# First exchange of q, k and softmax weights by ScalarE copies across partitions, and one store for a block's results

## The chip, the core and the metric

The kernel is one program on one core of a Trainium2 chip. The metric is device time in microseconds (us) of one execution, from launch to end; lower is better. Engines are named as in the profile: PE (TensorE, matmuls), PEld (its weight loads), DVE (VectorE), ACT (ScalarE), POOL (GpSimd), SP (SyncE, which here issues the DMAs).

## The reference, cut to what matters

```
scores = scale * q_c @ k_c^T          # chunks of 64 tokens; B=8, H=8, S=576, D=64
attn   = exp(scores - max) / (sum + 1e-9)
x      = (attn @ v_c)  -> (4608 tokens, 512)
h = x @ w_in;  g = h * sigmoid(1.702 h);  x = g @ w_out          # 512 -> 2048 -> 512
h = x @ w_in2; g = max(h,0) + alpha*min(h,0); out = g @ w_out2   # the same sizes
```

The weights come as 64-bit floats, which ACT and DVE turn into 32-bit ones, and every matmul operand of the feed-forward layers is split into a high and a low part by ACT, DVE and POOL; so these engines have a steady side job beside the matmuls.

## The kernel before, in words

The tokens are 36 groups of 128, nine blocks of 512. The program has two stages. In the first, up to about 525 us in the profile, the first feed-forward layer runs over the first five blocks as 80 steps n (five blocks times 16 slices of the hidden width). A step is 12 matmuls into `psH` (`emit_h`, L692, matmuls L699), the activation on ACT (L709), a rounded copy on ACT (L712), a subtraction on DVE (`gs`, L717), and two steps later 12 matmuls into `psY` (`emit_y`, L722, matmuls L729). Two `psH` buffers are in turn, so step n+2 can start only when the DVE subtraction of step n is done. Around these steps the attention of all later token groups and the preparation of the second layer's weights (lines L273 to L368) are threaded in by tables: every step has two half-slots, 2n in the middle of `emit_h` and 2n+1 after `emit_y`, and `put(half_slot, function, group)` decides what is issued there. All engines take their instructions in the order in which these functions issue them. In the second stage what remains of both layers runs as block products with seven multiplications (L699/L729 give way to L975 and L1123); it has its own tables (`GROUP_OP`, `LATE_0`, `LATE_STAGE`).

The place of the change is the attention of a token group with turn i. A group's q and k are loaded with 64 tokens of one half of the heads on 64 partitions (`load_nat`, L418); DVE transposes blocks of 32x32 (`qk_T`, L438, instructions L441) into a tile `ops` of 128 partitions x 2 halves x 768 columns (512 columns of q and k of group i, and 256 columns of the transposed softmax weights of the group two turns before, L610). Since a 32x32 transpose leaves half the data on the wrong 32 partitions, an exchange follows in three steps:

- `off_copy` (L449): ACT copies half 0 of `ops`, 128 x 768, aside into `off` (one buffer).
- `off_send` (L459): per 64 partitions, half 1 of the lower 32 partitions goes to half 0 of the upper 32. Two DMAs on SP, L463.
- `off_fetch` (L465): per 64 partitions, the upper 32 partitions of `off` go to half 1 of the lower 32. Two DMAs on SP, L469. It overwrites what `off_send` reads.

There are 30 such exchanges: 26 of 768 columns, two of 512 (turns 4 and 5) and two of 256. After it PE multiplies attention weights with v (`att_PV`, L640, 32 small matmuls into `psX`) and q with k of the next group but one (L538), both from the exchanged tile; ACT takes the product out (L654), DVE takes the maximum (L559, L561), ACT the exponential (L569, with a table load before and after, because the activation of L709 needs another table), DVE normalises (L577 to L582) and transposes (L610). In half-slots from the group's entry TAU: the maximum, exponential, normalising and transposing at 1, 1, 2, 2 (`ATT_AT`), the exchange of the tile two turns on at 3, 3, 4 (`OFF_AT`), and the product at TAU of the turn two later, mostly 8.

SP is one queue: it issues all DMAs in program order and stops at each that has to wait. At the end of a block `emit_y` takes four `psY` banks out (ACT L744, DVE L742, 128x512 each) into one tile `ysb` that is also the home of the next x, and stores each quarter by a DMA of its own into `x2d`, two at this half-slot and two at the next (`send_later`, issued at L295).

```
for fn, at in zip((off_copy, off_send, off_fetch), OFF_AT):
    put(t + at, fn, i + LAG)
put(pv, att_PV, g)
```

Of the kernel before, what the change touches and what calls it, by code (L numbers as in the profile page):

```python
# [17 lines left out]
SQ = 32  # L18
# [15 lines left out]

LAG = 2
LEAD = 3
TAU = (4, 10, 16, 22, 28, 32, 36, 40, 44, 48, 52, 56, 60, 64, 68, 72, 76, 80, 84, 88, 92, 96, 100, 104, 108, 112, 116, 120, 124, 128, 132, 136)
QK_T_AT = (18, 23)
OFF_FIRST = (1, 2, 4)
QK_4 = (4, 9)  # L40
ATT_FIRST = (-3, 1, 2, 5, 6, 7)
LO_POOL_O = (0, 0, 0, 1, 0, 0, 1, 0, 1, 1, 1, 1, 1, 0, 0, 1)
LO_POOL_I = (0, 0, 0, 1, 0, 1, 0, 0, 0, 0, 1, 0, 1, 1, 0, 0)
WI_DVE = (1, 0, 1, 0)
# [2 lines left out]
KEEP_WO = 0  # L47
KEEP_FROM = 10
KEEP_AT = 3
LATE_SEND = (1, 1)  # L50
SPLIT_AT = 3
XS_POOL = (0, 1, 1, 1)

END = (6, 9)
PREP_AT = (28, 33, 38, 43, 48, 53, 58, 63, 68, 73, 78, 83, 88, 93, 98, 103, 109, 114, 119, 124, 129, 134, 139, 143, 146)
FOLD_AT = (33, 36, 40, 44, 47, 50, 54, 57, 61, 63, 69, 72, 76, 79, 82, 85, 89, 93, 96, 100, 104, 107, 110, 113, 116, 119, 123, 127, 131, 134, 138, 141)
FOLD_SEND = 1
X1_SEND = 0
YSB_SEND = 0
PREP_STAGE = (0, 3, 4, 6, 9)  # L60
LATE_STAGE = (1, 5, 5, 8, 13)
ATT_AT = (1, 1, 2, 2)
OFF_AT = (3, 3, 4)
V_AT = 0
D_AT = 1
SUMS_AT = (43, 46, 71, 74)
X_HI_AT = (3, 8, 20, 24, 33, 36, 46)
FIRST_LOAD = 29
GROUP_OP = (27, 30, 34, 36, 43, 45, 47)
GROUP_SUM = (24, 32, 29, 38)  # L70
PREP_SEND = (0, 0)
LATE_0 = (90,)
LATE_2 = (8, 20, 34)
LATE_1 = (16, 46, 74)

# [25 lines left out]
def tile_chunk_attention_two_ffn(  # L101
# [14 lines left out]
    nc = tc.nc  # L116
    B, H, S, D = q.shape
    NT, DM = out.shape
    DFF = w_in1.shape[1]
    P = 128  # L120
    CH = 64
# [38 lines left out]
    x2d = [dram.tile([P, KT, NB], F32, name=f"x2_{j}") for j in range(NBLK)]  # L160
# [128 lines left out]
    def send_later(after=1, **dma):  # L289
        waiting.append((half + after, dma))  # L290
# [140 lines left out]
    ops_t, off_t = {}, {}  # L431
# [17 lines left out]
    def off_copy(k):  # L449
        if k < GPB + LAG:  # L450
            if k == GPB:
                off_t[k + 1] = raw_p.tile([P, 2, DW], F32, tag="raw2", name="off")
            off_t[k] = off_t[GPB + 1][:, k - GPB]
        else:
            off_t[k] = off_p.tile([P, DW + PW], F32, tag="off", name="off")
        c = cols(k) if k < len(GROUP_ORDER) else slice(DW, DW + PW)
        nc.scalar.copy(off_t[k][:, c], ops_t[k][:, 0, c])

    def off_send(k):  # L459
        t = ops_t[k]  # L460
        c = cols(k) if k < len(GROUP_ORDER) else slice(DW, DW + PW)
        for r in range(0, P, CH):
            nc.sync.dma_start(out=t[r + SQ:r + CH, 0, c], in_=t[r:r + SQ, 1, c])  # L463

    def off_fetch(k):  # L465
        t, o = ops_t[k], off_t[k]
        c = cols(k) if k < len(GROUP_ORDER) else slice(DW, DW + PW)
        for r in range(0, P, CH):
            nc.sync.dma_start(out=t[r:r + SQ, 1, c], in_=o[r + SQ:r + CH, c])  # L469

    qkT = {}

# [249 lines left out]
    def emit_y(n):  # L722
        j, f = divmod(n, NF)
        if f == 0:
            y_t[j] = [ps_y.tile([P, 512], F32, tag="y", name="psY") for _ in range(4)]
        gs, w = gs_t.pop(n), wt["wo", 0, f]
        for b, a in ((0, 0),) if n in Y_WHOLE else ((0, 0), (0, 1), (1, 0)):
            for t in range(4):
                nc.tensor.matmul(  # L729
                    y_t[j][t], w[:, a, t * P:(t + 1) * P], gs[:, b],  # L730
                    start=(f == 0 and a + b == 0), stop=(f == NF - 1 and b == 1),
                )
        if f == NF - 1:
            if j < NPL - 1:
                sbs = x_p.tile([P, 4, 512], F32, tag="x", name="ysb")
            for t, ps in enumerate(y_t.pop(j)):
                if j == NPL - 1:
                    sb = wpool.tile([P, 512], F32, tag=f"wo{8 + t}", name="ysb")
                else:
                    sb = sbs[:, t]  # L740
                if t % 2:
                    nc.vector.tensor_copy(sb, ps)  # L742
                else:
                    nc.scalar.copy(sb, ps)  # L744
                if j == NPL - 1:
                    nc.sync.dma_start(out=x2d[j][:, t], in_=sb)
                else:
                    send_later(YSB_SEND + t // 2, out=x2d[j][:, t], in_=sb)

# [172 lines left out]
    def second_layer():  # L924
# [27 lines left out]
        def split_soon():  # L952
            while unsplit:
                when = clock + (4 if clock < 14 else SPLIT_AT)
                at(when, split_factor, *unsplit.pop(0))
                at(when + KEEP_AT, keep_factors)

# [294 lines left out]
    with tc.manual_schedule():  # L1252
# [72 lines left out]
        for i, g in enumerate(GROUP_ORDER):  # L1325
            t = TAU[i]
            if i < GPB:
                for fn, at in zip((att_T, att_X, att_N, att_AT, att_PV), ATT_FIRST):
                    if i > 0 or fn is not att_T:
# [3 lines left out]
                if i == 0:  # L1333
                    put(t, att_S_matmuls, g)
                put(t + ATT_FIRST[5], load_v, GROUP_ORDER[i + 1])
                continue
            pv = TAU[i + LAG] if i + LAG <= last else TAU[last] + END[i + LAG - last - 1]
            before = QK_T_AT[i - GPB] if i < GPB + LAG else TAU[i - LAG] + D_AT
            put(before - LEAD, load_nat, g)
# [135 lines left out]
```

## Time and profile before

| | |
|---|---|
| median of three runs | 1555.92 us (1552.63 to 1559.21) |
| the profiled execution: its own time | 1560.17 us |
| its span, first to last instruction | 1558.4 us |
| PE busy | 1527.9 us, 98% |
| PEld busy | 1279.3 us, 82% |
| DVE busy | 1218.7 us, 78% |
| ACT busy | 955.5 us, 61% |
| POOL busy | 568.4 us, 36% |

The profiled execution is 4.25 us above the median of the runs; 1.8 us of its time lie outside the span. "Busy" of PE is the union of modelled matmul times.

### The profile page before, as it was taken

Reading aid. Unit: us, or ns where it says so; the run is one execution under the profiler, and the core shown is the slowest. Engines: PE = TensorE matmul, PEld = TensorE weight load, DVE = VectorE, ACT = ScalarE, POOL = GpSimd, SP = SyncE. Lnnn points to the kernel's source line nnn. Section 1 sums busy time; section 2 is a strip of 40 time slices with the busy share of each in tenths; the row PEclk is TensorE's granted clock in tenths of the full one; section 3 lists DMA queues with packets and bytes.
Section 4 is the critical chain, followed back from the end, with each engine's and each line's share of the span. In section 5 each row is a group of like instructions: output and inputs, shape, how many; then the busy total and the mean of one; then the engine's idle time right before and its main releaser. Section 6 shows DMA issues by size and latency. Waiting matters only on the chain.

```text
span 1558.4 us, 25552 instructions
## 1 busy us (share of the span) xinstructions
PE 1527.9 (98%) x9169; PEld 1279.3 (82%) x9169; DVE 1218.7 (78%) x1428; ACT 955.5 (61%) x1347; POOL 568.4 (36%) x542
## 2 busy tenths in 40 slices
PE   8999999999999999999999999999999999999998
PEld 6687777787888778888888787888888888999998
DVE  6998778676774659998899778777877788778777
ACT  6777666666674566666556665565655556556653
POOL 0135655666556222221111553225222422342330
PEclk9999999999999999999999999999999999999999
DMA  9925888899888477658665985689668866997985
GB/s 258 336 56 138 237 229 249 240 252 262 234 250 244 136 215 234 199 151 284 184 183 167 304 295 178 193 201 296 190 194 210 268 189 197 258 347 239 257 270 149
DMA packets 414958, 349.59 MB, mean 224 GB/s; under 512 B 139248, under 2 KB 337520, under 8 KB 414832
## 3 DMA queue, kind: packets, MB, share of 16 engines
q1 hardware_dynamic: 414832, 347.96, 75.6%
q8 instruction: 73, 1.20, 0.3%
q14 instruction: 53, 0.43, 0.1%
HBM read 257.70 MB, written 79.17 MB: 216 GB/s over the span
## 4 chain that ended last, share of the span: by engine, by line
PE 63%; DVE 6%; DMA 3%; POOL 2%; issue 2%; ACT 1%; SPq 1%; DVEq 0%; POOLq 0%; ACTq 0%
PE psYa L1123 16%; PE psHa L975 16%; PE psYb L1123 12%; PE psHb L975 12%; PE psY L729 3%; PE psH L699 3%; DVE o L1051 1%; DVE yacc L1161 1%; DMA wo<-fold 1%; DVE g L1026 1%; DVE w L874 1%; DMA wo<-u 1%; POOL fold L333 0%; POOL fold L364 0%; DMA ops<-ops 0%
## 5 line engine op out<-in xcount | busy, mean ns | idle before, releaser
L699 PE MATMUL psH<-xs,wi 128*128 128x512 f32 x960 | 234.9, 394 | 6.0 <-DVE gs L717 4.8
L729 PE MATMUL psY<-gs,wo 128*128 128x512 f32 x912 | 224.5, 396 | 1.1 <-DVE gs L717 1.1
L1123 PE MATMUL psYa<-o,w 128*128 128x512 f32 (+1 forms) x960 | 220.0, 377 | 1.8 <-DVE o L1051 1.6
L699 PEld LDWEIGHTS psH<-xs,wi 128*128 128x128 f32 x960 | 180.0, 189 | 48.4 <-DVE gs L717 7.2
L975 PE MATMUL psHa<-xop,wi2t 128*128 128x512 f32 (+1 forms) x948 | 214.1, 374 | 1.8 <-ACT g L1014 1.8
L1123 PEld LDWEIGHTS psYa<-o,w 128*128 128x128 f32 x960 | 176.5, 188 | 32.4 <-DVE o L1051 4.1
L729 PEld LDWEIGHTS psY<-gs,wo 128*128 128x128 f32 x912 | 169.8, 189 | 38.3 <-DVE gs L717 1.5
L975 PEld LDWEIGHTS psHa<-xop,wi2t 128*128 128x128 f32 x948 | 174.5, 188 | 29.4 <-ACT g L1014 2.2
L1123 PE MATMUL psYb<-o,w 128*128 128x512 f32 (+1 forms) x744 | 168.3, 374 | 0.4 <-DVE o L1051 0.4
L975 PE MATMUL psHb<-xop,wi2t 128*128 128x512 f32 (+1 forms) x744 | 167.1, 373 | 0.0
L990 ACT ACTIVATE neg<-g 128x1024 f32<-128x1024 f32 (+1 forms) x80 | 78.1, 976 | 126.0 <-DVE g L1026 125.3
L1123 PEld LDWEIGHTS psYb<-o,w 128*128 128x128 f32 x744 | 136.9, 188 | 22.0 <-DVE o L1051 0.8
L975 PEld LDWEIGHTS psHb<-xop,wi2t 128*128 128x128 f32 x744 | 136.8, 188 | 20.7
L1056 POOL TENSOR_TENSOR tsum<-g,tsum 128x1024 f32<-128x1024 f32 (+1 forms) x38 | 98.9, 2602 | 140.3 <-DVE o L1051 104.0
L1056 POOL TENSOR_TENSOR tsum<-g,g 128x1024 f32<-128x1024 f32 (+1 forms) x19 | 42.0, 2208 | 252.5 <-DVE g L998 252.5
L1161 DVE TENSOR_TENSOR yacc<-psYb,yacc 128x1024 f32<-128x1024 f32 (+1 forms) x73 | 83.2, 1139 | 40.5 <-PE psYb L1123 40.4
L1161 DVE TENSOR_TENSOR yacc<-psYa,yacc 128x1024 f32<-128x1024 f32 (+1 forms) x86 | 97.9, 1138 | 19.3 <-PE psYa L1123 19.3
L1051 DVE TENSOR_TENSOR o<-tsum,o 128x1024 fp32r<-128x1024 f32 (+1 forms) x61 | 71.5, 1171 | 52.3 <-ACT o L1046 52.1
L998 DVE SCALAR_TENSOR_TENSOR g<-g,neg 128x1024 f32<-128x1024 f32 (+1 forms) x80 | 101.0, 1263 | 9.4 <-ACT neg L992 9.4
L992 ACT ACTIVATE neg<-neg,minus_alpha 128x512 f32<-128x512 f32 (+1 forms) x160 | 100.2, 674 | 2.6
L1023 ACT COPY g<-psHa 128x1024 f32<-128x1024 f32 (+1 forms) x56 | 53.1, 949 | 78.1 <-DVE o L1051 49.9
L717 DVE TENSOR_TENSOR gs<-psH,gs 128x512 fp32r<-128x512 f32 x76 | 51.4, 678 | 62.6 <-ACT gs L712 62.5
(180 smaller groups left out, 2854.8 us busy)
## 6 DMA issues: line engine op xcount, KB each, us to landing
w<-wo SPq DMA_DIRECT2D x140, 512.0 KB, 4.1
wi2t<-wi SPq DMA_DIRECT2D x208, 256.0 KB, 3.8
w<-wi SPq DMA_DIRECT2D x72, 256.0 KB, 3.8
w<-wo SPq DMA_DIRECT2D x56, 256.0 KB, 3.1
raw<-in_moe_w_in_dram SPq DMA_DIRECT2D x16, 512.0 KB, 6.9
raw<-in_moe_w_out_dram SPq DMA_DIRECT2D x16, 512.0 KB, 7.3
raw<-in_moe_w_in_dram SPq DMA_DIRECT2D x32, 256.0 KB, 3.8
raw<-in_moe_w_out_dram SPq DMA_DIRECT2D x32, 256.0 KB, 4.7
```

Of the source, the lines that this page charges most:

```text
L699: nc.tensor.matmul(ps, w[:, a, c], xs[:, b, c], start=(i == 0), stop=(i == 3 * KT - 1))
L717: nc.vector.tensor_tensor(out=gs[:, 1], in0=g, in1=gs[:, 0].bitcast(F32), op=ALU.subtract)
L729: nc.tensor.matmul(y_t[j][t], w[:, a, t * P:(t + 1) * P], gs[:, b], start=(f == 0 and a + b == 0), stop=(f == NF - 1 and b == 1),)
L975: nc.tensor.matmul(ps, w[:, c, a], x[b][:, c], start=(k == 0 and i in (1, 2, 5)), stop=(k == 5 and i in (2, 3, 4)), skip_group_check=True,)
L990: nc.scalar.activation(out=neg, in_=src, func=AF.Relu, scale=-1.0)
L992: nc.scalar.activation(out=neg[:, jj], in_=neg[:, jj], func=AF.Copy, scale=minus_alpha[:, f + jj:f + jj + 1])
L998: nc.vector.scalar_tensor_tensor(out=g, in0=g, scalar=0.0, in1=neg, op0=ALU.max, op1=ALU.add)
L1023: nc.scalar.copy(g({1: "11", 6: "12", 5: "22"}[i]), src)
L1051: nc.vector.tensor_tensor(out=lo, in0=wide(homes[nm], n), in1=hi.bitcast(F32), op=ALU.subtract)
L1056: eng.tensor_tensor(out=wide(homes[out], n), in0=wide(homes[x], n), in1=wide(homes[y], n), op=ALU.subtract,)
L1123: nc.tensor.matmul(ps[:, d, :n], w[:, jj, d, a], x[b][:, jj], start=(k == 0 and i in (1, 5, 2)), stop=(k == 5 and i in (3, 2, 4)), skip_gr ...
L1161: nc.vector.tensor_tensor(out=out_acc, in0=ps[:, :, :n], in1=acc, op=ALU.add)
```

## The change

Three parts. `off_send` goes through a new helper `move`, and with SEND_BY "A" its two DMAs become two ACT copies of 32 partitions each, from partitions r to r+31 to partitions r+32 to r+63; `off_fetch` stays two DMAs on SP and `off_copy` one ACT copy. The four stores of a finished block (four of the first-stage blocks, so 16 DMAs of 256 KB) become one of 1 MB each (four DMAs), issued once the fourth quarter is out. And the tables are set anew: `off_send` moves from half-slot 3 to 4 (`OFF_AT`), the entries of turns 10 to 13 in `TAU` go from even to odd half-slots (52, 56, 60, 64 to 51, 55, 59, 63), and single entries of `QK_T_AT`, `ATT_FIRST`, `END`, `FOLD_AT`, `LATE_STAGE`, `GROUP_OP` and `LATE_0` move by one or two.

```diff
--- before.py
+++ after.py
@@ -34,11 +34,11 @@
 
 LAG = 2
 LEAD = 3
-TAU = (4, 10, 16, 22, 28, 32, 36, 40, 44, 48, 52, 56, 60, 64, 68, 72, 76, 80, 84, 88, 92, 96, 100, 104, 108, 112, 116, 120, 124, 128, 132, 136)
-QK_T_AT = (18, 23)
+TAU = (4, 10, 16, 22, 28, 32, 36, 40, 44, 48, 51, 55, 59, 63, 68, 72, 76, 80, 84, 88, 92, 96, 100, 104, 108, 112, 116, 120, 124, 128, 132, 136)
+QK_T_AT = (18, 24)
 OFF_FIRST = (1, 2, 4)
 QK_4 = (4, 9)
-ATT_FIRST = (-3, 1, 2, 5, 6, 7)
+ATT_FIRST = (-3, 1, 2, 5, 6, 8)
 LO_POOL_O = (0, 0, 0, 1, 0, 0, 1, 0, 1, 1, 1, 1, 1, 0, 0, 1)
 LO_POOL_I = (0, 0, 0, 1, 0, 1, 0, 0, 0, 0, 1, 0, 1, 1, 0, 0)
 WI_DVE = (1, 0, 1, 0)
@@ -47,29 +47,33 @@
 KEEP_WO = 0
 KEEP_FROM = 10
 KEEP_AT = 3
+SEND_BY = "A"
+FETCH_BY = "S"
+OFF_BY = "A"
+YSB_ONE = 1
 LATE_SEND = (1, 1)
 SPLIT_AT = 3
 XS_POOL = (0, 1, 1, 1)
 
-END = (6, 9)
+END = (5, 9)
 PREP_AT = (28, 33, 38, 43, 48, 53, 58, 63, 68, 73, 78, 83, 88, 93, 98, 103, 109, 114, 119, 124, 129, 134, 139, 143, 146)
-FOLD_AT = (33, 36, 40, 44, 47, 50, 54, 57, 61, 63, 69, 72, 76, 79, 82, 85, 89, 93, 96, 100, 104, 107, 110, 113, 116, 119, 123, 127, 131, 134, 138, 141)
+FOLD_AT = (33, 36, 40, 44, 47, 51, 54, 57, 61, 63, 69, 72, 76, 79, 82, 85, 89, 93, 96, 100, 104, 107, 110, 113, 116, 119, 123, 127, 131, 134, 138, 141)
 FOLD_SEND = 1
 X1_SEND = 0
 YSB_SEND = 0
 PREP_STAGE = (0, 3, 4, 6, 9)
-LATE_STAGE = (1, 5, 5, 8, 13)
+LATE_STAGE = (0, 5, 5, 8, 13)
 ATT_AT = (1, 1, 2, 2)
-OFF_AT = (3, 3, 4)
+OFF_AT = (3, 4, 4)
 V_AT = 0
 D_AT = 1
 SUMS_AT = (43, 46, 71, 74)
 X_HI_AT = (3, 8, 20, 24, 33, 36, 46)
 FIRST_LOAD = 29
-GROUP_OP = (27, 30, 34, 36, 43, 45, 47)
+GROUP_OP = (28, 30, 34, 36, 43, 44, 47)
 GROUP_SUM = (24, 32, 29, 38)
 PREP_SEND = (0, 0)
-LATE_0 = (90,)
+LATE_0 = (92,)
 LATE_2 = (8, 20, 34)
 LATE_1 = (16, 46, 74)
 
@@ -454,19 +458,25 @@
         else:
             off_t[k] = off_p.tile([P, DW + PW], F32, tag="off", name="off")
         c = cols(k) if k < len(GROUP_ORDER) else slice(DW, DW + PW)
-        nc.scalar.copy(off_t[k][:, c], ops_t[k][:, 0, c])
+        move(OFF_BY, off_t[k][:, c], ops_t[k][:, 0, c])
+
+    def move(by, out, in_):
+        if by == "S":
+            nc.sync.dma_start(out=out, in_=in_)
+        else:
+            {"A": nc.scalar.copy, "D": nc.vector.tensor_copy, "P": nc.gpsimd.tensor_copy}[by](out, in_)
 
     def off_send(k):
         t = ops_t[k]
         c = cols(k) if k < len(GROUP_ORDER) else slice(DW, DW + PW)
         for r in range(0, P, CH):
-            nc.sync.dma_start(out=t[r + SQ:r + CH, 0, c], in_=t[r:r + SQ, 1, c])
+            move(SEND_BY, t[r + SQ:r + CH, 0, c], t[r:r + SQ, 1, c])
 
     def off_fetch(k):
         t, o = ops_t[k], off_t[k]
         c = cols(k) if k < len(GROUP_ORDER) else slice(DW, DW + PW)
         for r in range(0, P, CH):
-            nc.sync.dma_start(out=t[r:r + SQ, 1, c], in_=o[r + SQ:r + CH, c])
+            move(FETCH_BY, t[r:r + SQ, 1, c], o[r + SQ:r + CH, c])
 
     qkT = {}
 
@@ -744,8 +754,11 @@
                     nc.scalar.copy(sb, ps)
                 if j == NPL - 1:
                     nc.sync.dma_start(out=x2d[j][:, t], in_=sb)
-                else:
-                    send_later(YSB_SEND + t // 2, out=x2d[j][:, t], in_=sb)
+                elif YSB_ONE:
+                    if t == 3:
+                        send_later(YSB_SEND, out=x2d[j], in_=sbs)
+                elif t % 2:
+                    send_later(YSB_SEND, out=x2d[j][:, t - 1:t + 1], in_=sbs[:, t - 1:t + 1])
```

How the order of instructions changes, at three places. First ACT, at the exchange whose copy aside the trace shows at 352.98 us; before (L457 is the copy aside, L321 a rounding of a prepared weight, L709 and L712 the activation and its rounded copy, L654 the product taken out, L569 the exponential and its table, L216 the first step of a weight's preparation):

```order
L457 COPY off<-ops 128x768
L321 CAST g<-u 128x384
L709 ACTIVATE psH<-psH 128x512
L712 CAST gs<-psH 128x512
L654 COPY x<-psX 128x4x64 x2
L569 ACT_TABLE_LOAD
L569 ACTIVATE e<-e 128x512
L216 ACTIVATE u<-raw_4160 128x512
L709 ACT_TABLE_LOAD
L709 ACTIVATE psH<-psH 128x512
```

And of the change, at the same place (L467 is the line in the helper, both for the copy aside and for the send; L325, L719, L722, L664, L579 and L220 are the lines above, 4 to 10 further down):

```order
L467 COPY off<-ops 128x768
L325 CAST g<-u 128x384
L719 ACTIVATE psH<-psH 128x512
L722 CAST gs<-psH 128x512
L664 COPY x<-psX 128x4x64 x2
L467 COPY ops<-ops 32x768 x2
L579 ACT_TABLE_LOAD
L579 ACTIVATE e<-e 128x512
L220 ACTIVATE u<-raw_4151 128x512
L719 ACT_TABLE_LOAD
L719 ACTIVATE psH<-psH 128x512
```

Two copies of 32x768 stand between the product taken out and the table load of the exponential; nothing else moved on ACT here.

Then SP at the same exchange, before (L463 the send, L469 the fetch, L283 a weight's load, L295 stores, L407 the load of v):

```order
L283 DMA raw_4160<-in_moe_w_in_dram 128x2x128 x2
L463 DMA ops<-ops 32x768 x2
L295 DMA wi_6_147<-g 128x3x128
L295 DMA wi_6_147<-u 128x3x128
L407 DMA v<-in_v_dram 128x8x64
L469 DMA ops<-off 32x768 x2
L295 DMA wo_0_125<-fold 896x1x128
```

And of the change (L465 is the helper's line, here the fetch):

```order
L287 DMA raw_4151<-in_moe_w_in_dram 128x2x128 x2
L299 DMA wi_6_147<-g 128x3x128
L299 DMA wi_6_147<-u 128x3x128
L411 DMA v<-in_v_dram 128x8x64
L465 DMA ops<-off 32x768 x2
L299 DMA wo_0_125<-fold 896x1x128
```

The send's two DMAs are gone; the queue comes to the stores, v and the fetch directly from the weight's load.

Last PE, at the products of turns 9 to 11; before (L699 a step's first matmuls, L729 its second, L640 and L538 the attention):

```order
L699 MATMUL psH<-xs,wi 128x512 x12
L640 MATMUL psX<-ops,v 64x64 x16
L538 MATMUL psX<-ops 64x64 x16
L729 MATMUL psY<-gs,wo 128x512 x12
L699 MATMUL psH<-xs,wi 128x512 x12
L729 MATMUL psY<-gs,wo 128x512 x12
L699 MATMUL psH<-xs,wi 128x512 x12
L640 MATMUL psX<-ops,v 64x64 x16
L538 MATMUL psX<-ops 64x64 x16
L729 MATMUL psY<-gs,wo 128x512 x12
L699 MATMUL psH<-xs,wi 128x512 x12
```

And of the change (L709, L739, L650 and L548 in their place):

```order
L709 MATMUL psH<-xs,wi 128x512 x12
L650 MATMUL psX<-ops,v 64x64 x16
L548 MATMUL psX<-ops 64x64 x16
L739 MATMUL psY<-gs,wo 128x512 x12
L709 MATMUL psH<-xs,wi 128x512 x12
L739 MATMUL psY<-gs,wo 128x512 x12
L650 MATMUL psX<-ops,v 64x64 x16
L548 MATMUL psX<-ops 64x64 x16
L709 MATMUL psH<-xs,wi 128x512 x12
L739 MATMUL psY<-gs,wo 128x512 x12
L709 MATMUL psH<-xs,wi 128x512 x12
```

From the second product on (entry 51 in place of 52) the attention's matmuls stand ahead of the 12 matmuls of a step that they stood behind; so it is for four turns.

## Rows read from the trace of the kernel before

**Rows 1.** Who PE waited for, 160 to 364 us: total us, times, longest

```profile
PE psX L640 <- DMA ops<-off: 4.5, 6, 1.5
PE psX L640 <- DMA wi<-u: 1.1, 1, 1.1
PE psY L729 <- DVE gs L717: 1.1, 1, 1.1
PE psX L640 <- DVE d L579: 0.9, 1, 0.9
PE psH L699 <- DVE gs L717: 0.9, 2, 0.6
PE psX L640 <- DMA x<-xg: 0.6, 1, 0.6
```

**Rows 2.** PE in order of time: start, us, what, [idle before, releaser]

```profile
183.16 0.80 PE L640 MATMUL psX<-ops,v 64*64 64x64 f32 x30 [1.09 <-DMA wi<-u]
...
220.93 0.83 PE L640 MATMUL psX<-ops,v 64*64 64x64 f32 x30 [0.92 <-DVE d L579]
...
363.52 0.87 PE L640 MATMUL psX<-ops,v 64*64 64x64 f32 x30 [1.49 <-DMA ops<-off]
...
521.36 2.25 PE L699 MATMUL psH<-xs,wi 128*128 128x512 f32 x6 [2.70 <-DVE gs L717]
```

**Rows 3.** SP in order of time: start, us of issuing, what

```profile
178.63 1.24 SPq L469 DMA_DIRECT2D ops<-off  x2
...
215.89 1.73 SPq L407 DMA_DIRECT2D v<-in_v_dram  x2
217.70 1.31 SPq L469 DMA_DIRECT2D ops<-off  x2
...
356.26 1.23 SPq L463 DMA_DIRECT2D ops<-ops  x2
...
360.01 1.15 SPq L469 DMA_DIRECT2D ops<-off  x2
```

**Rows 4.** The sends' line L463: ns of one issue min/median/max; landing

```profile
L463 SPq DMA_DIRECT2D ops<-ops x60: 512/588/1453, 91.3 to 475.4; - x60
...
DMA to landing us min/median/max: 2.0/3.1/6.6
```

**Rows 5.** The fetches' line L469: landing, us after issue

```profile
DMA to landing us min/median/max: 2.1/2.9/4.8
```

**Rows 6.** What SP waited for, 90 to 490 us: total us, times, longest

```profile
SPq L469 <- DMA ops<-ops: 15.2, 15, 2.2
```

**Rows 7.** Busy time by stretch: us, PE, PEld, DVE, ACT, POOL, PEclk, DMA

```profile
365.20:368.50 3.30, 3.30 (x9) 2.64 (x8) 2.77 (x5) 3.27 (x6) 3.14 (x7) 0.50 0.98 282
368.60:372.00 3.40, 3.40 (x16) 2.81 (x15) 2.86 (x6) 1.26 (x1) 2.87 (x5) 1.00 0.73 207
```

**Rows 8.** ACT copies by shape: xcount, busy us, mean ns, idle before and releasers

```profile
L457 ACT COPY off<-ops 128x768 f32<-128x768 f32 x26 | 21.7, 836 | 46.7 <-DVE ops L610 31.1 <-DMA ops<-off 14.4 <-DVE u L224 0.9
...
L744 ACT COPY ysb<-psY 128x512 f32<-128x512 f32 x10 | 5.4, 596 | 6.9 <-PE psY L729 6.9
...
L1203 ACT COPY x_b<-psHa 96x512 f32<-96x512 f32 x2 | 1.2, 582 | 8.7 <-PE psHa L1195 8.4 <-DMA out_dram<-g 0.3
```

**Rows 9.** Who ACT waited for, 90 to 490 us: total us, times, longest

```profile
ACT off L457 <- DVE ops L610: 31.1, 11, 4.4
ACT u L216 <- DMA raw<-in_moe_w_in_dram: 17.3, 10, 4.3
ACT off L457 <- DMA ops<-off: 15.7, 9, 4.4
ACT e L569 <- DVE e L561: 11.8, 18, 2.6
```

**Rows 10.** ACT in order of time

```profile
355.22 0.66 ACT L654 COPY x<-psX 128x256 f32<-128x256 f32 x2
...
359.89 0.67 ACT L216 ACTIVATE u<-raw 128x512 f32<-128x512 f32 x1 [1.86 <-DMA wi<-g]
```

## The prediction

> **What bounds the kernel now.** I read the busy times first: PE works in 1527.9 of 1558.4 us, so at most 30.5 us of waiting can be had, and no change to a side engine does more. Then I read what ended PE's waits in the stretch of the exchanges. The reader is to see in [rows 1] that 4.5 us in six waits ended with a landing of the fetch (`ops<-off`), all at L640, the product with v. Three more waits at L640 (1.1, 0.9 and 0.6 us) carry other names, a store of a weight, a reciprocal and a store of x, which that product does not read. The order in time clears them up: the product at 220.93 starts 3.2 us after the fetch issued at 217.70, that at 183.16 starts 4.5 us after the one at 178.63 [rows 2, 3], and fetches land 2.1 to 4.8 us after their issue [rows 5]. So I count all of them as waits for the exchange: 4.5 + 1.1 + 0.9 + 0.6 = 7.1 us, at eight products. What else PE waits for there is `gs`, DVE's subtraction behind ACT's activation: 1.1 + 0.9 = 2.0 us [rows 1].
>
> Why is the fetch late? There are two reasons, seen in SP's order. At 356.26 the send is issued, and the fetch follows at 360.01 although stores and v need only part of that time: it overwrites what the send reads, so it stands until the send has landed. 15 of the 30 exchanges wait like this [rows 3, 6]. The other half are late because the queue is: at 217.70 the fetch starts just as v's two issues (215.89 + 1.73 us) end [rows 3].
>
> The longest of these waits, 1.49 us at 363.52, has a second price: the granted clock is 0.50, the 1.2 GHz level, from 365.2 to 368.5, with 9 matmuls in 3.30 us where the stretch behind it, at 2.4 GHz, has 16 in 3.40 [rows 2, 7]. At that rate 15.5 would have been done; 6.5 x 3.40 / 16 = 1.4 us are lost.
>
> **The send on ACT: what it takes away.** Gone are 60 issues on SP of 588 ns [rows 4], 35 us of the queue, 1.18 us per exchange, and the landing in the middle of the chain. Up to now it takes an issue (0.6 us) and 3.1 us from the second issue to the landing [rows 4], 3.7 us; two ACT copies take its place. The shape 32x768 is not in the trace; 128x768 takes 836 ns, and on fewer partitions a copy is not quicker: 96x512 takes 582 ns, 128x512 596 ns [rows 8]. So a pair costs 2 x 0.836 = 1.67 us; below this I have no row, and I take it. The chain shortens by 3.7 - 1.7 = 2.0 us where the send's landing was waited for, more than the longest wait there (1.49 us); where the queue was late it comes 1.18 us earlier, more than the longest of the three waits with other names (1.1 us). So I take all 7.1 us back, and with the long wait the 1.4 us of clock: 8.5 us.
>
> The Trainium skill would give a little less. Its page "SBUF — State Buffer" (The DMA setup-cost knee) has a transfer cost a fixed 2 us or so plus its bytes over 436 GB/s; for 96 KB my estimate by it is 2.2 us. By this the chain would shorten by 0.6 + 2.2 - 1.7 = 1.1 us, 0.4 us of the longest wait would stay and the clock might still fall, and the sum below would come out at 1550.9 us. [rows 4] has 3.1 us, and I go by it.
>
> **What it adds.** ACT gets 26 x 1.67 us, twice 2 x 0.59 us, and two pairs of 256 columns that cost no more: about 48 us more, all between 90 and 490 us. Queued behind a pair are the exponential, then the activation of the next step; DVE waits for both, to normalise and for `gs`, and PE for `gs`. What covers it are ACT's own waits in that stretch: 31.1 us for DVE's transposes, 17.3 for loads of weights, 15.7 for the one `off` buffer, which the fetch frees (so they shrink with it), and 11.8 us for the exponential's input, right behind the new copies [rows 9]: 75.9 us against 48. The exchange at 356.26 shows it: ACT takes the product out until about 355.9, the pair would follow, and the load waited for at 359.89 leaves 1.86 us idle, so ACT is level again there [rows 10]. Where the cover is gone, a wait for `gs` grows by a pair. Lower bound 0; upper bound, all three waits for `gs` of [rows 1] longer by 1.67 us, 5.0 us. Most of the time ACT waits again within a step, so I take one of them, 1.7 us.
>
> **Tables and block stores.** With turns 10 to 13 one half-slot earlier, two products (turns 10 and 11) stand 12 matmuls, 12 x 3.40 / 16 = 2.6 us [rows 7], nearer to an exchange that was not moved, and two (turns 14 and 15) as much farther. The bounds are a wait of 1.49 us for each of the two, 3.0 us, and the same gained on the other two. Zero, because the chain is 1.2 to 2.0 us shorter for the first two. The block stores leave 12 issues, 7 us of SP by [rows 4] over four block ends; the one store waits for the last quarter, and that holds the queue by about one 596 ns copy each [rows 8]. Zero: no wait in [rows 1] names these stores. Where the load of v is put later (`ATT_FIRST`) it is one half-slot in the first four turns, whose entries (4 to 22) lie before all waits counted; zero. The second stage's entries move by one or two; nothing I found ties a wait of PE to them, so zero, with 1.5 us either way, as much as the longest wait for the exchange.
>
> **Sum.** -7.1 - 1.4 + 1.7 = -6.8 us. The profiled execution's 1560.17 us would become 1553.4; it lies 4.25 us above the median, so against 1555.92 us I forecast 1549.1 us.
>
> **Rivals.**
> - *The queue stays late.* The sends' landing goes, but SP falls behind for its other loads, and PE, quicker now, comes earlier to the same fetches. Half of 7.1 us stays: -3.5 - 1.4 + 1.7 = -3.2, 1552.7 us. For it: half of the fetches did not wait for the send [rows 6]. Against it: 1.18 us of queue per exchange. The Trainium skill, "DMA: Bandwidth & Descriptors" (Issuing engines are not separate DMA queues), speaks for this rival: the time to initiate a DMA is usually small beside the DMA itself. Here it is 588 ns against 3.1 us, a fifth [rows 4].
> - *SP's relief reaches farther.* Weights and q, k land earlier, ACT's 17.3 us of waiting for them shrink [rows 9], and the 2.0 us on `gs` go too, at no price on ACT: -8.5 - 2.0 = -10.5, 1545.4 us. With the 2.70 us at 521.36 [rows 2], where the first stage ends, 1542.7. For it: ACT and SP are both waiting on each other's lateness. Against: DVE is the busier engine, and the change gives it nothing.
> - *Slower: ACT becomes the bound.* Between 120 and 360 us every pair delays exponential, normalising, transposes and the next `gs` in turn, and PE waits 1.67 us per uncovered exchange. It passes the 8.5 us gained and the measurement's 0.5% (7.8 us) at (8.5 + 7.8) / 1.67, 10 of 30 exchanges. With 18 of them it is 30.1 - 8.5 = +21.6, 1577.5 us. For it: PE already waits on `gs` three times there. Against: the 75.9 us of ACT's waits.
> - *No more than tables*: the product's wait is in truth for something that the change leaves; then the price on ACT alone is left, 1557.6 us.
>
> **How the numbers follow.** A measurement of this kernel tells about 0.5%, 7.8 us, from no change; the bound lies at 1548.1 us, inside the forecast's own range of 1547.4 (no price on ACT) to 1552.4 (the upper one). Chances: forecast 0.45, of which 0.21 beyond the bound, since the tables may take back a little more than I give them; queue stays late 0.23; farther relief 0.19; slower 0.09; nothing 0.04. So faster 0.21 + 0.19 = 0.40, same 0.24 + 0.23 + 0.04 = 0.51, slower 0.09. The range goes from 1541, a little below 1542.7 for the second stage's 1.5 us, to 1559, above 1557.6 for the same: it leaves out the slower rival and about 0.05 below.
>
> **What would show it.** Right: no wait at L640's new line longer than 0.3 us after 160 us; granted clock 1.00 around 365 us; ACT busy 48 us more; the copies of 32x768 near 0.84 us; fetches issued within 2.5 us of the copy aside's end where the queue is free. Wrong: waits for `gs` together above 6 us between 100 and 360 us (ACT is the bound), or waits at the product of more than 3 us with fetches issued right behind other DMAs (the queue is), or copies of 32 partitions far from 0.84 us.

## The result, and the profile after

The changed kernel takes 1540.74 us (median of 4 runs, 1539.37 to 1542.40) against 1555.23 us for the kernel before beside it: ratio 0.9905, 95% interval 0.9881 to 0.9929. Two later comparisons gave 0.9922 (0.9896 to 0.9948) and 0.9923 (0.9905 to 0.9941). The forecast was 1549.1 us, the range 1541 to 1559: the time lies 0.3 us below the range, and the gain of 14.5 us is about twice the forecast 6.8.

The profiled execution after took 1541.47 us. PE's waits from 160 to 364 us, to be read against [rows 1] (total, times, longest):

```profile
PE psX L650 <- DVE u L234: 2.2, 1, 2.2
PE psH L709 <- DVE gs L727: 0.7, 1, 0.7
PE psX L650 <- DMA ops<-off: 0.5, 1, 0.5
```

The waits of 7.1 us at eight products with v have become two of 2.8 us. The long one stands at 169.78 us; it ends as the fetch lands, and VectorE's `u` is named only because it ended at the same time. The granted clock, 0.50 around 366 us before [rows 7], is now 1.00:

```profile
360.00:366.00 6.00, 6.00 (x28) 4.97 (x27) 5.19 (x10) 5.89 (x9) 4.82 (x8) 1.00 0.83 226
```

The send's copies (count, ns of one min/median/max), the landing of the fetches at L465 after their issue, and the largest sum of SP's waits between 90 and 490 us (total, times, longest):

```profile
L467 ACT COPY ops<-ops x60: 402/832/838, 92.8 to 466.6; 32x768 f32<-32x768 f32 x52, 32x512 f32<-32x512 f32 x4, 32x256 f32<-32x256 f32 x4
```

```profile
DMA to landing us min/median/max: 2.0/3.4/4.8
```

```profile
SPq L465 <- ACT ops L467: 22.0, 23, 4.5
```

The copy's price was read rightly (832 ns against 836). The estimate of 2.2 us for 96 KB by the Trainium skill's "SBUF — State Buffer" (The DMA setup-cost knee) stays short here: the median fetch took 3.4. The fetch, though, still stands in SP's queue for the pair: 23 times, at 15 of the 30 exchanges, 22.0 us in all, where it stood 15 times, at 14 exchanges, 15.2 us for the send [rows 6]. What got shorter is seen in the exchange whose product waited 1.49 us before [rows 2]. ACT and SP in order of time, first before, then after:

```profile
352.98 0.83 ACT L457 COPY off<-ops 128x768 f32<-128x768 f32 x1 [3.56 <-DVE ops L610]
```

```profile
345.83 0.83 ACT L467 COPY off<-ops 128x768 f32<-128x768 f32 x1 [3.44 <-DVE ops L620]
...
348.75 1.69 ACT L467 COPY ops<-ops 32x768 f32<-32x768 f32 x2
...
349.61 1.43 SPq L465 DMA_DIRECT2D ops<-off  x2
...
354.82 0.69 PE L650 MATMUL psX<-ops,v 64*64 64x64 f32 x32
```

From the copy aside to the fetch it was 360.01 - 352.98 = 7.0 us [rows 3] and is 349.61 - 345.83 = 3.8 us; the median of all 30 exchanges went from 7.3 to 5.2 us. The fetch can start behind the first of the two copies; it needn't see a landing any more. PE reaches the product without a wait.

The gain that the forecast did not count lies where the first stage gives way to the second, near 521 us before. VectorE, SP and GpSimd there, before:

```profile
499.34 1.20 SPq L283 DMA_DIRECT2D raw<-in_moe_w_out_dram  x2
500.59 0.60 SPq L817 DMA_DIRECT2D x_b<-x  x1
...
515.73 4.97 DVE L874 TENSOR_TENSOR w<-w 128x512 fp32r<-128x512 f32 x5
515.95 1.61 POOL L325 TENSOR_TENSOR sums<-sums,g 128x512 fp32r<-128x512 f32 x1 [4.23 <-ACT g L321]
520.62 0.68 DVE L717 TENSOR_TENSOR gs<-psH,gs 128x512 fp32r<-128x512 f32 x1
```

And after:

```profile
487.23 1.21 SPq L287 DMA_DIRECT2D raw<-in_moe_w_out_dram  x2
488.48 0.60 SPq L830 DMA_DIRECT2D x_b<-x  x1
...
503.21 3.08 DVE L887 TENSOR_TENSOR w<-w 128x512 fp32r<-128x512 f32 x5
505.66 1.79 POOL L329 TENSOR_TENSOR sums<-sums,g 128x512 fp32r<-128x512 f32 x1 [6.46 <-ACT g L325]
506.22 0.68 DVE L727 TENSOR_TENSOR gs<-psH,gs 128x512 fp32r<-128x512 f32 x1
```

(A split takes the low part of a weight, L874 before and L887 after; the sums are GpSimd's side job of preparing weights.) Before, VectorE's five splits of `w` run beside GpSimd's sums and take 4.97 us; after, they are nearly done when the sums begin, and take 3.08. Counted from the first matmul of the same step (484.06 us before, 473.78 after), the last weight's load is issued at 15.28 us before and 13.45 after and the splits start at 31.67 and 29.43, while the sums start at 31.89 and 31.88. So the splits' lead over the sums grew from 0.22 to 2.45 us. Before, `gs` behind them keeps PE waiting 2.70 us [rows 2]; after, no wait of PE is there, and the 0.50 clock near 522 us is gone with it. The Trainium skill, "SBUF — State Buffer" (SBUF: two separate sides), says that VectorE with two SBUF inputs and GpSimd lock each other out of a port pair for a whole instruction; the 4.97 and 3.08 us agree with that.

### The profile page after: what moved, and what is told of

It is laid out like the page before. It is cut to its first block, busy times and chain, and to the rows that moved or that the text cites. A ratio compares the mean times of both kernels' runs of the same rounds, so it can differ in the third digit from the quotient of the medians.

```text
span 1539.7 us, 25515 instructions
## 1 busy us (share of the span) xinstructions
PE 1519.2 (99%) x9167; PEld 1274.7 (83%) x9169; DVE 1215.5 (79%) x1428; ACT 1004.4 (65%) x1407; POOL 565.9 (37%) x542
## 4 chain that ended last, share of the span: by engine, by line
PE 81%; DVE 4%; ACT 2%; DMA 1%; issue 1%; SPq 0%; ACTq 0%; DVEq 0%
PE psYa L1136 17%; PE psHa L988 17%; PE psYb L1136 13%; PE psHb L988 12%; PE psY L739 10%; PE psH L709 9%; PE psX L650 1%; DVE yacc L1174 1%; PE psX L548 1%; DVE o L1064 0%; DVE g L1039 0%; DMA raw<-in_moe_w_in_dram 0%; DMA ops<-off 0%; DVE tsum L1069 0%; DVE op3l L1064 0%
## 5 line engine op out<-in xcount | busy, mean ns | idle before, releaser
L709 PE MATMUL psH<-xs,wi 128*128 128x512 f32 x960 | 233.6, 393 | 3.3 <-DVE gs L727 1.2
L739 PE MATMUL psY<-gs,wo 128*128 128x512 f32 x912 | 221.8, 393 | 0.0
L709 PEld LDWEIGHTS psH<-xs,wi 128*128 128x128 f32 x960 | 178.4, 188 | 44.6 <-DVE gs L727 3.1
L739 PEld LDWEIGHTS psY<-gs,wo 128*128 128x128 f32 x912 | 169.1, 188 | 36.1
L1036 ACT COPY g<-psHa 128x1024 f32<-128x1024 f32 (+1 forms) x56 | 53.2, 950 | 77.5 <-DVE o L1064 48.9
L1064 DVE TENSOR_TENSOR o<-g,o 128x1024 fp32r<-128x1024 f32 (+1 forms) x62 | 90.8, 1464 | 0.8 <-ACT o L1059 0.8
```

The lines of the kernel that those rows point to most:

```text
L709: nc.tensor.matmul(ps, w[:, a, c], xs[:, b, c], start=(i == 0), stop=(i == 3 * KT - 1))
L739: nc.tensor.matmul(y_t[j][t], w[:, a, t * P:(t + 1) * P], gs[:, b], start=(f == 0 and a + b == 0), stop=(f == NF - 1 and b == 1),)
L1036: nc.scalar.copy(g({1: "11", 6: "12", 5: "22"}[i]), src)
L1064: nc.vector.tensor_tensor(out=lo, in0=wide(homes[nm], n), in1=hi.bitcast(F32), op=ALU.subtract)
```

## The experiments

The table sums PE's waits over 0.15 us in each profiled execution: those at the product with v, all others from 100 to 485 us, and those from 485 us to the second stage. Under "w" stands how long the five splits of `w` took at the end of the first stage, under "lead" how long before the next work of GpSimd the first of them starts (below 0, GpSimd is already at work).

| kernel | median us | ratio (95%) | product | other | end | w | lead |
|---|---|---|---|---|---|---|---|
| before | | | 7.1 | 3.7 | 3.4 | 4.97 | 0.22 |
| changed | 1540.74 | 0.9905 (0.9881-0.9929) | 2.8 | 2.3 | 0 | 3.08 | 2.45 |
| after_again | 1542.61 | 0.9922 (0.9896-0.9948) | 2.6 | 2.3 | 0 | 3.08 | 2.31 |
| after_third | 1541.65 | 0.9923 (0.9905-0.9941) | 1.9 | 2.2 | 0 | 3.08 | 1.43 |
| send_only | 1544.23 | 0.9947 (0.9932-0.9962) | 1.9 | 4.1 | 0 | 3.09 | 2.50 |
| send_ysb | 1543.91 | 0.9944 (0.9924-0.9964) | 1.0 | 3.5 | 0 | 3.09 | 2.12 |
| ysb_only | 1551.69 | 0.9994 (0.9977-1.0011) | 6.1 | 2.7 | 3.2 | 4.70 | 0.97 |
| new_sched_only | 1601.91 | 1.0315 (1.0290-1.0340) | 42.6 | 1.6 | 0 | 3.09 | 1.98 |
| sched_off_old | 1551.35 | 0.9987 (0.9969-1.0005) | 7.0 | 2.5 | 3.2 | 4.97 | 0.41 |
| slot_only | 1608.96 | 1.0344 (1.0325-1.0363) | 39.9 | 1.8 | 0 | 3.09 | 2.77 |
| last_only | 1546.98 | 0.9957 (0.9942-0.9973) | 3.4 | 2.9 | 0 | 3.09 | 2.39 |
| all_but_last | 1544.60 | 0.9941 (0.9917-0.9964) | 1.6 | 3.6 | 0 | 3.09 | 2.04 |
| prep_early | 1557.11 | 1.0023 (1.0013-1.0034) | 4.9 | 3.8 | 6.2 | 5.76 | -0.24 |
| raw_two_early | 1558.54 | 1.0021 (1.0006-1.0037) | 7.0 | 3.9 | 3.5 | 5.00 | -0.13 |
| xb_ahead | 1556.03 | 1.0005 (0.9990-1.0021) | 11.3 | 3.2 | 3.7 | 4.97 | 0.21 |
| act_twice | 1556.15 | 1.0017 (1.0003-1.0032) | 5.1 | 5.8 | 3.8 | 4.98 | 0.14 |
| fetch_act | 1552.07 | 0.9987 (0.9975-0.9999) | 1.8 | 11.4 | 0 | 3.09 | 2.21 |
| send_actq | 1553.45 | 1.0000 (0.9989-1.0010) | 1.4 | 8.7 | 3.6 | 4.97 | 0.12 |
| send_dve | 1541.26 | 0.9909 (0.9893-0.9925) | 0 | 5.7 | 0 | 3.09 | 2.35 |
| send_split | 1541.04 | 0.9917 (0.9898-0.9935) | 1.1 | 3.0 | 0 | 3.09 | 2.18 |

**Which part of the change pays.** Edits against the kernel before, as values of the changed kernel's switches ("S" and 0 stand for the code of before; only the lines that matter are shown):

```diff
# send_only
-SEND_BY = "S"
+SEND_BY = "A"
-OFF_AT = (3, 3, 4)
+OFF_AT = (3, 4, 4)
# ysb_only
-YSB_ONE = 0
+YSB_ONE = 1
# new_sched_only: all tables of the change, SEND_BY = "S", YSB_ONE = 0
# send_ysb: send_only and ysb_only together
```

> Only the sends go to ScalarE (the table that says when, OFF_AT, with them); every other table and the four stores a block are those of before. The forecast's theory, that the change acts through the waits of the PV product at L650 and through the sends alone: those waits and the 0.50 clock stretch near 365 us go, about 7 to 8 us, so 1547 to 1549; the wait of 2.70 us before gs near 521 us and the 0.50 stretch behind it stay. The theory that a relieved SP queue also brings the weight loads forward: 1541 to 1543, with no wait over 1 us near 521. The theory that the other tables (END above all) take away the wait near 521: 1546 to 1549, and the wait is still there.

> Only the one store in place of four for each finished block; sends by DMA and all tables of before. The forecast: no change, 1555.2 within 1 us. The theory that SP's queue counts everywhere: three issues fewer a block, some 0.6 us each, bring loads and fetches forward near the block ends, so 1 to 4 us faster, 1551 to 1554. The theory of the tables: no change.

> Only the tables of the change, with the sends by DMA and four stores a block. The forecast: no change by themselves, 1555.2 within 1 us. The theory that END and its companions take away the wait near 521 us: about 5 us faster, 1550 to 1551, no wait over 1 us there. If steps set half a slot earlier only pay with the sends on ScalarE, the waits at the PV product grow and it is slower: 1556 to 1560.

> The sends on ScalarE and the one store, with the tables of before except OFF_AT. The forecast: as with the sends alone, 1547 to 1549. The theory of the SP queue: 1540 to 1542, all of the change's gain. The theory of the tables: 1546 to 1549, with the wait near 521 us still there.

The sends alone bring 0.53%, 8.2 us of 1554.33, and with them the wait near 521 us goes, though `END` is the old one: it is not the tables' doing. In send_only PE waits from 100 to 540 us:

```profile
PE psX L650 <- DMA ops<-off: 1.9, 1, 1.9
PE psY L739 <- DVE gs L727: 1.7, 1, 1.7
PE psH L709 <- DVE gs L727: 1.2, 2, 0.6
PE psH L709 <- POOL xs L687: 0.7, 1, 0.7
PE psH L709 <- ACT wo L188: 0.5, 1, 0.5
```

The store can't be told from nothing. The tables without the sends cost 3.2%, far beyond what any theory had: the product waits 23 times for the fetch and twice, by the profile, for v.

```profile
PE psX L650 <- DMA ops<-off: 21.6, 23, 4.8
PE psX L650 <- DMA v<-in_v_dram: 11.5, 2, 5.9
```

**Which table, and what tables give behind the sends.**

```diff
# slot_only (kernel before)
-OFF_AT = (3, 3, 4)
+OFF_AT = (3, 4, 4)
# sched_off_old: new_sched_only with
-OFF_AT = (3, 4, 4)
+OFF_AT = (3, 3, 4)
# after_again, after_third: the changed kernel
```

> The tables of the change but OFF_AT, with the sends by DMA at the slot of before and four stores. If the 47 us of the tables with DMA sends come from OFF_AT alone (the send asked for one slot later, with the fetch): about 1555, within 2 us. If they come from the five steps set half a slot earlier (TAU 51 to 63), they stand between 180 and 290 us alone: 1560 to 1575.

> The kernel before with only OFF_AT (3, 4, 4): the DMA send is asked for one slot later, in the slot of its fetch; sends by DMA, all other tables and the stores as before. If the 47 us that the tables cost with DMA sends are this slot's: 1590 to 1605, waits at L650 in most exchanges. If it needs the five earlier steps as well: 1560 to 1580.

> The changed kernel again, to have it beside parts of it on one chip with a narrower interval: 1539 to 1542. If the tables other than OFF_AT give nothing once the sends are on ScalarE, its ratio agrees with that of the sends and the one store with the old tables (0.9944); if they give 3 us, 0.990 to 0.992.

> The changed kernel once more, beside the split pair on one chip and to narrow its interval against the kernel before: 1540 to 1543, ratio 0.990 to 0.993; gs waits of 2 to 3 us between 100 and 485 us and no wait over 1 us near 521 us, as in its two profiles so far.

The slot is all of it. A DMA send asked for in the slot of its fetch leaves its landing nowhere to hide (3.4% alone); with the old slot the other tables cost nothing. So the later slot goes only with the copies by ScalarE; whether the copies need it is not shown, for no run has them at the old slot. PE's wait in slot_only:

```profile
PE psX L650 <- DMA ops<-off: 25.0, 28, 3.3
```

Behind the sends, the other tables may give something: the 16 runs of the changed kernel average 1541.6 us (standard deviation 2.0), the 19 of send_only and send_ysb 1544.3 (2.3). The difference is 2.7 us, its interval twice the root of 2.0²/16 + 2.3²/19, 1.5 us. The runs of the two were on several chips, so this is weaker than a ratio, and by the ratios (0.9905 to 0.9923 against 0.9944 and 0.9947) the intervals overlap: not shown. It fits the traces: the wait of psY for `gs` (1.7 us in send_only) is in none of the changed kernel's three profiles.

**Where the sends must go.** Sends on ScalarE for some exchanges only, which have the later slot of `OFF_AT` with them; the other tables of before:

```diff
-            move(SEND_BY, t[r + SQ:r + CH, 0, c], t[r:r + SQ, 1, c])
+            move(SEND_BY if ACT_SEND(k) else "S", t[r + SQ:r + CH, 0, c], t[r:r + SQ, 1, c])
# last_only: ACT_SEND = lambda k: k > 28     all_but_last: k < 29
```

> Sends on ScalarE for the last three exchanges alone (in the kernel before their sends stand at 456, 465 and 475 us); 27 sends by DMA, all other tables and the four stores as before. The theory that SP's relief at the end of the first stage takes the wait of 2.70 us before gs near 521 us away: 4 to 6 us faster, 1548.5 to 1550.5, that wait gone, the waits at L650 between 160 and 365 us still there. The theory that the gain is at the PV product alone, and that the wait near 521 went for other reasons: no change, 1554 to 1556, that wait still there.

> The complement: the first 27 exchanges send on ScalarE, the last three by DMA. The theory that the two gains are separate: the waits at L650 go and the wait near 521 us stays, 3 to 5 us faster, 1549.5 to 1551.5. The theory that the PV product is all: 1543 to 1546, as with all sends on ScalarE.

The edit moved more than the expectations say. Exchanges count from 4 to 33, so `k > 28` takes the last five, and the trace of last_only has ten send copies:

```profile
L467 ACT COPY ops<-ops x10: 402/830/834, 420.6 to 468.9; 32x768 f32<-32x768 f32 x6, 32x256 f32<-32x256 f32 x4
```

In last_only the first theory's signs came true: the wait near 521 us went and the waits at the product before 365 us stayed (3.2 us). That the two gains are separate fell in all_but_last, where the wait near 521 us went too. The last five sends bring 6.7 us and the other 25 bring 9.2, together 15.9, where all 30 bring 8.2; the excess of 7.7 us is clear of its interval, about 5 us by the three intervals of the table. The 3.4 us near 521 us and their clock stretch are in neither half's profile, so they are counted in both. This wait is not a sum but a threshold: the five splits of `w` take 4.70 to 5.76 us in all eight profiles of the table that show the wait, and 3.08 or 3.09 in the twelve without it. In the twelve they start at least 1.43 us ahead of GpSimd's next work, in the eight at most 0.97 us ahead. A microsecond or two on the way there decides.

**What sets that wait.** Sends by DMA, loads moved (kernel before):

```diff
# prep_early
-PREP_AT = (..., 129, 134, 139, 143, 146)
+PREP_AT = (..., 129, 133, 138, 142, 145)
# raw_two_early
+PREP_AT = (..., 129, 134, 138, 142, 146)
# xb_ahead
-                x_load(0, "b22")
+                x_load(0, "b22"); x_load(0, "b21")
             if to_go == 7:
-                x_load(0, "b21")
+                pass
```

> The kernel before with the last four weight loads of the first stage asked for one slot earlier (about 3 us); all sends by DMA on SP. The theory that the wait near 521 us comes of the last raw load landing some 2 to 4 us late, with VectorE's work piling up behind it: that wait shrinks to under 1 us with its clock stretch, 4 to 6 us faster, 1548.5 to 1550.5. The theory that it needs fewer issues on SP, not an earlier place: no change, 1553 to 1556.

> The kernel before, all sends by DMA on SP; of the last four weight loads only the second and third to last are asked for one slot earlier (139 to 138, 143 to 142), the last stays at 146, so that it isn't ahead of the loads of x for the second stage. The theory that the wait near 521 us comes of the whole last chain on SP (third load, its split on VectorE, last load, last load of x) being 2 us late, which puts VectorE's seven splits of w beside GpSimd's sums: last load of x issued as in the faster kernels (about 2 us earlier against the matmuls), splits 4.2 us in place of 6.1, no wait over 1 us there, 4 to 6 us faster, 1548 to 1550. The theory that only fewer DMAs on SP do it: no change, 1552 to 1555.

> The kernel before, all sends by DMA on SP; only the last load of x for the second stage is issued right behind the one before it, ahead of the last weight load. The theory that the load of x alone sets the splits' start: 4 to 6 us faster, 1548 to 1550, no wait near 521 us. The theory of the whole chain: the last weight load then lands 0.6 us later and ScalarE still meets it first, so the wait shrinks by less than 1 us and the time is 1552 to 1555.

My theory that a late load or chain of loads can be mended by its place fell three times. Asking for weights earlier puts other DMAs behind them: in prep_early ScalarE meets the load of x later, and PE's wait grows to 5.4 us. In xb_ahead the loads of x come first on SP, but the last weights are no earlier than before against the matmuls, and the splits take 4.97 us:

```profile
502.57 0.95 SPq L830 DMA_DIRECT2D x_b<-x  x2
504.33 1.27 SPq L287 DMA_DIRECT2D raw<-in_moe_w_out_dram  x2
```

So none of these other orders did it. Fewer DMAs on SP are not the rule either: send_actq (below) takes 60 off SP and keeps the wait, and new_sched_only and slot_only have all 60 on SP and don't show it. In these two PE itself is more than 40 us later, and the splits start 2.0 and 2.8 us ahead of the sums; in slot_only:

```profile
566.48 3.09 DVE L887 TENSOR_TENSOR w<-w 128x512 fp32r<-128x512 f32 x5
569.25 1.48 POOL L329 TENSOR_TENSOR sums<-sums,g 128x512 fp32r<-128x512 f32 x1 [6.78 <-ACT g L325]
```

What goes with the wait in all 20 profiles is the splits' lead, and the relief of SP is one way to it. That the splits' slowing comes of GpSimd is read from their times side by side; no kernel took GpSimd's sums away, and that stays open.

**The price on ScalarE, and other engines.** Against the changed kernel, but send_actq against the one before:

```diff
# act_twice: each send copy issued twice
# fetch_act
-FETCH_BY = "S"
+FETCH_BY = "A"
# send_dve
-SEND_BY = "A"
+SEND_BY = "D"
# send_split
+            move("D" if r else "A", t[r + SQ:r + CH, 0, c], t[r:r + SQ, 1, c])
# send_actq: the sends as nc.scalar.dma_start in place of nc.sync.dma_start
```

> The changed kernel with every send copy issued twice, the second writing the same values again: 60 copies more on ScalarE, +48 us busy. The forecast's price, an exchange on ScalarE hidden under its waits but for one gs wait a pair longer (+1.7 us): 1542 to 1546. The rival that ScalarE becomes the bound when some 10 of 30 exchanges lie uncovered: each doubled pair costs up to 1.67 us, 10 of them +17 us, 1555 or more. Nothing at all: 1540 to 1542.

> The changed kernel with the fetches on ScalarE too (two copies of 0.84 us in place of two DMAs that land 3.4 us after issue). If SP's queue still holds anything back: the last wait at L650 (2.2 us near 170 us) goes, 1536 to 1540. If ScalarE's cover is spent (its waits for the product's operands were 17 us after the change, against +48 us more): slower, 1545 to 1560.

> The kernel before with the sends still DMAs, but issued from ScalarE's queue and not SP's. The theory that the gain is SP's queue (60 issues of 0.59 us and the waits of the fetch behind them): most of the gain of the ScalarE copies, 1544 to 1548, no wait over 1 us near 521 us. The theory that the gain is the copy's speed (1.67 us against a landing of 3.1 us): the PV product's waits at L650 stay as in the kernel before, 1552 to 1556.

> The changed kernel with the send copies on VectorE in place of ScalarE (in the window from 160 to 480 us VectorE is busy 238 us and ScalarE 257). If what an engine pays for the pair is what stands behind it in order (gs is made on VectorE last, just ahead of the matmuls that wait for it): gs waits grow as with fetches on ScalarE, 1548 to 1556. If the copies are hidden on either engine: 1540 to 1544.

> The changed kernel with the pair of send copies shared: the first on ScalarE, the second on VectorE, so that both run at once and neither engine has more than 0.84 us an exchange in front of gs. If the price of a pair is the time that it stands before gs in one engine's order: the wait of 2.2 us near 170 us (ScalarE) and the gs waits of 0.9 us near 142 and 163 us (VectorE) both shrink, 1538 to 1540. If what is left has other causes: 1540 to 1542, as with either engine.

The first pair per exchange is nearly free, the next is not: act_twice, with ScalarE busy 43.9 us more (1004.4 to 1048.3), costs 1556.15 - 1541.65 = 14.5 us (on two chips; the ratios, 1.0017 and 0.9923, say the same). Not all of this is ScalarE's order, for the fetch waits for the doubled copies too: SP stands 42.3 us for them in place of 22.0. PE in act_twice, 100 to 540 us:

```profile
PE psH L709 <- DVE gs L727: 8.7, 8, 2.7
PE psX L650 <- DMA ops<-off: 3.5, 4, 1.8
```

The wait near 521 us is back, with as few DMAs on SP as after the change: the last weight's load is issued 15.3 us after the first matmul of its step, as late as before, and the lead is 0.14 us. With the fetches on ScalarE (44.1 us more busy) the product hardly waits any more, but `gs` eats it up; by the ratios, 0.9987 against 0.9923, it costs about 10 us, and the other waits grew by 9.2:

```profile
PE psH L709 <- DVE gs L727: 8.5, 7, 2.1
```

send_actq takes the same 60 issues off SP and gains nothing: the product's waits fall to 1.4 us, but ScalarE, which now holds the queue, pays it back at `gs`: 8.7 us of other waits up to 485 us where the kernel before had 3.7. The Trainium skill, "DMA: Bandwidth & Descriptors" (Issuing engines are not separate DMA queues), says that another engine to issue from saves only the sequencer time; the ratio of 1.0000 agrees. On VectorE the copy takes as long as on ScalarE, and the product's last wait goes:

```profile
L467 DVE COPY ops<-ops 32x768 f32<-32x768 f32 x50 | 41.9, 839 | 5.8 <-ACT off L467 4.7
```

The other waits are longer by about as much (5.7 us against 2.3), so the time is that of the changed kernel. The split pair is not faster either: 1541.04 us beside 1541.65 on one chip. No version tried beats the changed kernel by more than the runs' spread.

## Why the prediction missed

By its steps:

- *The product's waits, -7.1 us.* The mechanism was right and the size too high: 7.1 us became 2.8, 2.6 and 1.9 in three profiles, so 4.3 to 5.2 us. The step that each exchange comes earlier by more than its wait fails near 170 us: PE arrives 1.9 us earlier than before, but the fetch, issued 1.65 us earlier behind other DMAs on SP, lands no earlier (the first of its two DMAs at 169.4 us before, 169.6 after), and 1.7 to 2.2 us stay. One profile doesn't fix the 7.1 either: up to 410 us last_only, prep_early, raw_two_early and xb_ahead are the same program as the kernel before, and they have 3.4, 4.5, 5.3 and 11.3 us there. The 15 waits of the fetch, read as 15 exchanges, are at 14; one exchange waits twice.
- *The clock, -1.4 us.* The stretch near 365 us is gone, as said. It was partly this execution's luck: of the five profiles of that same program only this one and xb_ahead have it, and neither ysb_only nor sched_off_old does.
- *ACT's price, +1.7 us.* Others than product and end: 2.7 to 3.9 us in the five profiles with DMA sends on SP and the old tables or only loads moved, 2.5 with the new tables and DMA sends (sched_off_old); 4.1, 3.5 and 3.6 with the sends, or all but five of them, on ScalarE and the old tables; 2.2 or 2.3 after. So the sends cost about 1 us at most, not clear of the spread, and the tables, taken at zero, seem to take that back. The argument for it, 75.9 us of ScalarE's waits as cover for 48, was too generous: the next 44 us cost 10 (fetch_act) to 14.5 (act_twice). Cover shrinks as a queue elsewhere gets faster: ScalarE's waits for weights fell from 17.3 us [rows 9] to 4.1.
- *The step that failed: the end of the first stage at zero.* The sum left out the 2.70 us at 521.36 [rows 2], and gave the second stage's tables zero within 1.5 us. From a matmul of the first stage (484.06 us before, 473.78 after) to the second stage's first (539.40 and 523.59) it took 55.3 us and takes 49.8, 5.5 less: 3.4 of waits, and 1.7 for the clock stretch, in which 12 matmuls take 4.61 us where the steps around take 2.88. (The stretch is this execution's: sched_off_old, act_twice and send_actq have the same wait of 2.7 us without one.) Added to the -6.8 of the sum that makes -12.3; with what the two profiles show for the other terms, -4.3 - 1.4 - 1.4 - 5.5 = -12.6. The three comparisons say -14.5, -11.2 and -12.0 (1555.23 - 1540.74 and so on). The rival "SP's relief reaches farther" had this, 2.70 us and all, and its 1542.7 us was the best number in the text; it had a chance of 0.19. Part of that is luck: it took all of 7.1 us at the product and left out the clock near 522 us, two errors against each other. I put it lower because the wait stands on `gs`, VectorE's, and "the change gives it nothing". What I didn't do is follow VectorE back from that wait: ahead of its splits it waits 4.1 us for ScalarE's rounding of x, ScalarE 4.8 us for a weight and 0.9 for x, which SP had issued late, and so the splits ran beside GpSimd and were slow.
- *The span overstates.* The two profiled spans differ by 18.7 us: 2.9 us of that is in the second stage, 1.3 in the opening (a clock stretch at 24 us that one of the changed kernel's three profiles has as well).
- *The marks.* Copies at 0.84 us, ACT busy 48.9 us more (955.5 to 1004.4), clock 1.00: right. No wait over 0.3 us at the product after 160 us: wrong at two. Fetches within 2.5 us of the copy aside's end: too hopeful, 349.61 - (345.83 + 0.83) = 2.95 us in the exchange shown, where the pair stands behind two casts, an activation and a copy of ScalarE's, and above 2.5 us in all 30.

## What to carry to other kernels

When DMAs leave a queue, follow every wait of the bound engine back to what that queue issued, also far from the edit; at this stage's end, where several engines are level, a threshold was hidden that a microsecond or two decides. Two parts that both remove the same wait each get the credit for it alone, so parts that add up to more than the whole are the sign of such a threshold. Moving a load earlier in the full queue here only changed which load was late, and idle time of a helper engine is no budget: the first 49 us were nearly free, the next 44 cost 10 to 14.5. And a term read from one profile is as good as its spread: the same program waited 3.4 to 11.3 us at the product.

## What the runs showed of the hardware

- Five of VectorE's two-input operations of 128x512 took 3.08 us when they started 1.43 us or more ahead of GpSimd's work, also where the last of them overlapped it by 1.66 us (after_third), and 4.70 to 5.76 us when they started at most 0.97 us ahead. GpSimd's sums of 128x128 took 0.79 to 0.91 us there before; their median in the whole kernel is 0.46, the longest 1.32.
- A copy of 32x768 took 832 ns on ScalarE and 839 ns on VectorE, as long as one of 128x768 on ScalarE, 836 ns [rows 8].
- The kernel before spreads from 1547 to 1560 us over its runs, the changed one from 1538 to 1545. The five profiles of the same program up to 410 us, with 3.4 to 11.3 us at the product, show one source of it.
